# Attention with a threshold and a mixing block on one core: a re-priced plan, joined value products, reciprocals spread through DRAM

## The chip, the cores and the metric

The kernel runs on one core of a Trainium2 chip. The metric is device time in microseconds (us) for the whole program. The core has TensorE (matrix products and transposes, PE in the profile; its weight loads are PEld), VectorE (DVE), ScalarE (ACT), GpSimd (POOL) and SyncE (SP), which here only issues DMAs. Results of TensorE land in PSUM banks; everything else on the chip is in SBUF.

## The reference

Two stages, one behind the other (shapes: 8 batches, 8 heads, 576 positions, 64 per head, so 512 channels):

```python
scores = scale * np.matmul(q, k.transpose(0, 1, 3, 2))
thresh = np.max(scores, axis=-1, keepdims=True) - tau
scores = np.where(scores >= thresh, scores, -1000000000.0)
scores = scores - np.max(scores, axis=-1, keepdims=True)
attn = np.exp(scores)
attn = attn / (np.sum(attn, axis=-1, keepdims=True) + 1e-09)
x = attn @ v                       # heads side by side: 8 x 576 x 512
theta = x @ w_theta
zr = x * np.cos(theta); zi = x * np.sin(theta)
u = x + w_tok_r @ zr + w_tok_i @ zi
out = u + np.maximum(u @ w_ch, 0.0)
```

The weights come in double precision; w_theta and w_tok_i are about five times larger than a usual draw, so the angles need accuracy.

## The kernel before

**Work.** Heads are taken two at a time: 32 pairs, four to a batch. A pair has nine units of 128 rows of scores: four for each head and one that holds the last 64 rows of both (the "tails"). For a unit TensorE makes the scores (s_ps, 128 x 576) from query and key, each split into a high and a low term of a reduced fp32 form (fp32r); VectorE empties them with a minus sign and takes the row minimum (L511), ScalarE takes the exponential (L529), VectorE applies the threshold and sums the rows (L537). TensorE turns the result in blocks of 128 x 128 (t_ps, L572 and L607), ScalarE copies the turned blocks into the tiles a0 (the tails and the first two units of each head, 320 columns) and a1 (256 columns), and TensorE multiplies them with v (o_ps, L650): one run of 20 instructions for a0 in the middle of the pair, one for a1 at its end. ScalarE copies both into x, transposed (xT, channels by positions).

**Normalizing.** The nine columns of row sums of a pair become reciprocals on VectorE (L672, L673). ScalarE spreads eight of them, each over 64 columns (rb, L677); TensorE turns them in four blocks (rb_ps, L685) and the ninth in another (rl_ps, L691), and VectorE multiplies x by what stands in these two banks (L697, and L703 twice).

**Mixing.** For each batch: x is split (xh, xl); the angles are four products of 24 instructions (m_ps, L775); VectorE takes whole turns off; ScalarE makes cosine and sine (L855, L856), for which it loads another table and loads the old one back; GpSimd multiplies by x; TensorE turns z (z_ps, L885), and the token product runs over 4 x 54 instructions (y_ps, L933). Then u is split and multiplied with w_ch (m_ps again).

**Weights.** At the start each block of weights is turned from double precision into a high and a low fp32r term: VectorE works on the bits (L254 to L272), and the low term comes out of TensorE as a sum of three products (w_ps, L301 twice and L302): the bits and a correction w, both as fp32 against an identity (or one divided by a whole turn), minus the high term. There are 8 pieces of 512 columns (w_theta and w_ch) and 18 of 288 (w_tok). The terms of w_theta and w_ch go to DRAM and are read back for each batch (wm).

**Order.** The order on every engine is fixed before the program runs. A planner (class Plan) holds all pieces of work with an engine, a time, what they need, the buffers they take and a rank. It lets time pass: on the engine that can start first it takes, of the works that can start then, the one with the lowest rank. Ranks are counted in steps of 3.2 us a unit, with fixed offsets (a score at h - 3, an exponential at h - 2). Buffers are counted in pots: six PSUM banks, one pair of banks for the scores, three tiles for two units' scores (s2), one each of a0 and a1, three raw tiles. SP issues the DMAs of query, key, their copies (qq, kd, tails), v, weights and outputs in one queue; query and key of a pair are cast on ScalarE after the query was scaled there (L393), the low terms come from GpSimd (for the first pair from VectorE). Each engine runs its list in order, so an instruction that waits holds up all behind it.

## Time and profile before

| | |
|---|---|
| median of 3 runs | 1081.22 us (1077.72 to 1082.82) |
| profiled execution | 1080.86 us, its span 1078.8 us |
| TensorE, VectorE, ScalarE, GpSimd busy | 95%, 74%, 62%, 21% of the span |
| mean granted clock of TensorE | 0.995 |
| DMA engines busy | 49.9% of 16 engines' span |

The span runs from the first to the last instruction of the execution that the profiler recorded; the 2 us beside it lie outside. Matrix products are pipelined: the profile shows the length of one from its own begin to its own end, so what one costs in a row of many is read from the distance between starts.

### The profile page before, as it was taken

How to read it: one execution, taken by the hardware profiler on the slowest of the kernel's cores; microseconds unless marked ns; L12 is line 12 of the kernel's file. 1: busy time of each engine (PE TensorE's matmuls, PEld its weight loads, DVE VectorE, ACT ScalarE, POOL GpSimd, SP SyncE). 2: the span in 40 equal slices, each digit the busy share in tenths (PEclk: the TensorE clock that was granted, in tenths of full speed). 3: DMA queues.
4: the chain of work that ended last, by engine and by line, in shares of the span. 5: the costliest groups of instructions: out<-in, count | busy, mean ns of one | idle time of the engine just before them, and what ended most of it. 6: DMA issues, size and time to landing. Idle time of an engine off the chain costs nothing.

```text
span 1078.8 us, 21076 instructions
## 1 busy us (share of the span) xinstructions
PE 1022.4 (95%) x7650; PEld 905.0 (84%) x7650; DVE 800.1 (74%) x2152; ACT 669.9 (62%) x1269; POOL 231.1 (21%) x162
## 2 busy tenths in 40 slices
PE   4889899998999999999899999999999998999998
PEld 2667688888789988888788987999788888899898
DVE  5998887877777786776777777766877778776572
ACT  5878867645775558655685566754586556854250
POOL 1111232312332014211241123320142212320100
PEclk9999999999999999999999999999999999999999
DMA  8877455556634563346642366444544466421411
GB/s 259 211 211 188 125 135 145 133 161 161 178 89 101 149 168 101 97 101 182 174 117 71 98 187 168 100 101 136 161 118 101 100 180 178 110 59 38 132 54 64
DMA packets 81799, 144.05 MB, mean 134 GB/s; under 512 B 26272, under 2 KB 34464, under 8 KB 81696
## 3 DMA queue, kind: packets, MB, share of 16 engines
q1 hardware_dynamic: 81696, 142.71, 49.9%
q8 instruction: 61, 1.00, 0.4%
q14 instruction: 42, 0.34, 0.1%
HBM read 72.42 MB, written 13.63 MB: 80 GB/s over the span
## 4 chain that ended last, share of the span: by engine, by line
PE 76%; DVE 8%; ACT 7%; DMA 5%; SPq 2%; issue 2%; POOL 0%; ACTq 0%; POOLq 0%; DVEq 0%
PE y_ps L933 22%; PE o_ps L650 13%; PE s_ps L497 12%; PE m_ps L775 12%; PE t_ps L572 9%; PE z_ps L885 3%; DMA qraw<-in_qT_dram 2%; DVE sc L511 2%; PE w_ps L301 2%; DMA kd<-khl 2%; SPq L217 2%; DVE xl L214 1%; PE t_ps L607 1%; DVE s_sb L537 1%; PE rb_ps L685 1%
## 5 line engine op out<-in xcount | busy, mean ns | idle before, releaser
L537 DVE SCALAR_TENSOR_TENSOR s_sb<-sc,nm,s_sb 128x576 f32<-128x576 f32 x288 | 247.1, 863 | 97.8 <-ACT s_sb L529 95.6
L529 ACT ACTIVATE s_sb<-sc,nm 128x576 f32<-128x576 f32 x288 | 223.6, 786 | 85.3 <-DVE sc L511 84.5
L511 DVE TENSOR_SCALAR_CACHE_REDUCE sc<-s_ps 128x576 f32<-128x576 f32 x288 | 216.9, 753 | 57.7 <-PE s_ps L497 56.2
L583 ACT COPY a<-t_ps 128x512 f32<-128x512 f32 x256 | 147.7, 590 | 99.6 <-PE t_ps L572 99.0
L497 PE MATMUL s_ps<-kd,qq 128*128 128x288 f32 x1024 | 186.1, 303 | 22.9 <-DVE sc L511 22.3
L497 PEld LDWEIGHTS s_ps<-kd,qq 128*128 128x128 f32 x1024 | 147.7, 188 | 35.8 <-DVE sc L511 32.1
L572 PE MATMUL t_ps<-ident,s_sb 128*128 128x128 f32 x1152 | 171.9, 274 | 4.5 <-DVE s_sb L537 4.5
L650 PE MATMUL o_ps<-a,v 128*64 128x256 f32 (+1 forms) x1280 | 170.2, 412 | 0.0
L933 PE MATMUL y_ps<-wt_l,zh 128*128 128x288 f32 x576 | 168.0, 308 | 0.0
L933 PE MATMUL y_ps<-wt_h,zh 128*128 128x288 f32 x576 | 163.5, 304 | 0.1
L572 PEld LDWEIGHTS t_ps<-ident,s_sb 128*128 128x128 f32 x1152 | 139.8, 141 | 8.3 <-DVE s_sb L537 6.4
L214 POOL TENSOR_TENSOR qhl<-qraw,qhl 128x576 fp32r<-128x576 f32 x31 | 46.4, 1497 | 460.6 <-ACT qhl L397 380.4
L650 PEld LDWEIGHTS o_ps<-a,v 128*64 128x64 f32 x1280 | 87.8, 137 | 61.2 <-issue 10.6
L933 PE MATMUL y_ps<-wt_h,zl 128*128 128x288 f32 x576 | 114.0, 306 | 0.0
L933 PEld LDWEIGHTS y_ps<-wt_l,zh 128*128 128x128 f32 x576 | 108.1, 189 | 3.7 <-issue 3.7
L933 PEld LDWEIGHTS y_ps<-wt_h,zh 128*128 128x128 f32 x576 | 107.1, 189 | 0.4 <-ACT zh L891 0.4
L775 PE MATMUL m_ps<-xh,wm 128*128 128x288 f32 x512 | 93.1, 307 | 11.3 <-ACT a L583 10.4
L868 POOL TENSOR_TENSOR z<-z,xT 128x576 f32<-128x576 f32 x56 | 78.2, 1432 | 83.4 <-ACT z L855 83.4
L775 PE MATMUL m_ps<-uh,wm 128*128 128x288 f32 x512 | 92.2, 302 | 0.3 <-DVE uh L211 0.3
L933 PEld LDWEIGHTS y_ps<-wt_h,zl 128*128 128x128 f32 x576 | 85.6, 189 | 6.1 <-issue 6.1
L775 PEld LDWEIGHTS m_ps<-xh,wm 128*128 128x128 f32 x512 | 76.0, 193 | 17.1 <-ACT a L583 11.8
L775 PEld LDWEIGHTS m_ps<-uh,wm 128*128 128x128 f32 x512 | 74.6, 188 | 4.3 <-issue 3.8
(88 smaller groups left out, 1440.1 us busy)
## 6 DMA issues: line engine op xcount, KB each, us to landing
wm<-wm_dram SPq DMA_DIRECT2D x64, 512.0 KB, 4.0
kd<-khl SPq DMA_DIRECT2D x64, 288.0 KB, 4.3
qq<-qhl SPq DMA_DIRECT2D x128, 128.0 KB, 2.4
kd<-khl SPq DMA_DIRECT2D x64, 256.0 KB, 4.1
v<-in_vp_dram SPq DMA_DIRECT2D x32, 320.0 KB, 2.9
qraw<-in_qT_dram SPq DMA_DIRECT2D x32, 288.0 KB, 4.4
kraw<-in_kT_dram SPq DMA_DIRECT2D x32, 288.0 KB, 4.7
out_dram<-xT SPq DMA_DIRECT2D x32, 288.0 KB, 4.5
```

The lines of the kernel that those rows point to most:

```text
L214: eng.tensor_tensor(out=out, in0=a, in1=b, op=ALU.subtract)
L497: nc.tensor.matmul(ps.tile[:, half, :HS], st, kk[:, half * HS : (half + 1) * HS], start=(x == 0), stop=(x == len(terms) - 1),)
L511: nc.vector.tensor_scalar(out=sc.tile.rearrange("p (a b) -> p a b", a=2), in0=ps.tile[:, :, :HS], scalar1=-1.0, scalar2=None, op0=ALU.mult ...
L529: nc.scalar.activation(out=u.s.tile[:, j], in_=sc.tile, func=AF.Exp, bias=nm.tile[:, 0:1], scale=-1.0)
L537: nc.vector.scalar_tensor_tensor(out=e, in0=sc.tile, scalar=nm.tile[:, 1:2], in1=e, op0=ALU.is_le, op1=ALU.mult, accum_out=pr.rows.tile[:, ...
L572: nc.tensor.transpose(out=bank.tile[:, c * P : (c + 1) * P], in_=sf[:, k0 + c * P : k0 + (c + 1) * P], identity=ident)
L583: nc.scalar.copy(out=t.a[:, :, j, q0 : q0 + P], in_=bank.tile.rearrange("p (c q) -> p c q", c=4))
L650: nc.tensor.matmul(bank.tile[64 * j : 64 * j + 64, :w], st, mv, start=(c == 0), stop=(c == 4))
L775: nc.tensor.matmul(banks[h].tile[:, :HS], wm.tile[:, a, c, :], x[:, h * HS : (h + 1) * HS], start=(key == 0), stop=(key == 11),)
L868: eng.tensor_tensor(out=zi, in0=zi, in1=xs[m].x.tile, op=ALU.mult)
L885: nc.tensor.transpose(out=bank.tile[:, i * P : (i + 1) * P], in_=z.tile[:, c : c + P], identity=ident)
L933: nc.tensor.matmul(bank.tile[:, :HS], st, (wt_l if wl else wt_h)[:, c, hs], start=(k + q == 0), stop=(k + q == 26),)
```

## The change

- **Planner.** A DMA can start only when at most seven before it are under way (RING), its own time and landing are counted apart; works on VectorE and GpSimd marked "shared" don't run at the same time; each engine may take a work that starts up to SLACK later if its rank is lower; a work may be released before its forerunner's end where only its issue or its first half is needed; times are other numbers throughout. The fixed offsets of ranks are replaced by a table (LEAD). Weights have earlier ranks and closer steps than before.
- **Values.** Both products of a pair are one run of 40 instructions at the pair's end, with two banks. A tile a0 or a1 is taken when the first block is turned for it, not when it is copied.
- **Normalizing.** The nine columns of reciprocals are turned at once (r_ps, 9 x 128), copied to SBUF (rinv), written to DRAM in three DMAs (rows_dram) and read back in two, each over 64 partitions (rb, 128 x 576). One multiplication on VectorE from SBUF takes the place of three.
- **Weights.** The correction w is written as fp32r and multiplied with an fp32r identity. The products of the first batch's token mixing wait for all of w_tok.
- **Start.** The first pair's tails come by two DMAs from ScalarE's queue and are split on ScalarE and VectorE; key is loaded ahead of query; the exponential's table is loaded at once.
- **Scaling.** The factor of the scores sits in VectorE's emptying (scalar1=gate) and no longer in a pass over the query on ScalarE.

```diff
+RING = 8
+SLACK = {"PE": 0.05, "DVE": 0.1, "ACT": 0.1, "POOL": 0.1, "SP": 0.8}
+
+LEAD = dict(
+    score=-4.74, empty=-29.63, offset=-10.18, power=-8.2, mask=12.6, flip=0.34, evict=-7.42, flip5=-4.13,
...
                 first, starts = NEVER, []
+                base = free[e] if e != "SP" else max(free[e], sent[-RING])
                 for w in wait[e]:
-                    at = max(free[e], w.ready)
+                    at = max(base, w.ready)
+                    if w.shared:
+                        at = max(at, port[other[e]])
...
-                    best = (first, min((x for x in starts if x[0] <= first + 1e-6), key=lambda x: x[1].rank)[1])
+                    best = min((x for x in starts if x[0] <= first + SLACK[e]), key=lambda x: x[1].rank)
...
-    PACE, TURN_PACE = 0.131, 0.109
+    PACE, TURN_PACE = 0.1335, 0.109
...
-    nc.vector.tensor_scalar(out=gate, in0=tau_sb, scalar1=0.0, scalar2=1.0 / root, op0=ALU.is_ge, op1=ALU.mult)
+    nc.vector.tensor_scalar(out=gate, in0=tau_sb, scalar1=0.0, scalar2=-1.0 / root, op0=ALU.is_ge, op1=ALU.mult)
...
+    tail_raw = const.tile([P, P], F32, name="tail_raw")
+    nc.gpsimd.memset(tail_raw, 0.0)
+    for j in range(2):
+        r = slice(64 * j, 64 * j + 64)
+        nc.scalar.dma_start(tail_raw[r, r], qT[0, 0, j, :, 512:])
+    nc.scalar.preload_act_table(AF.Exp)
...
+        unit = (turns, turns_r) if turn else (ident, ident_r)
...
-                t.w = get(holds.w, [P, S], F32, "w")[:, :n]
+                t.w = get(holds.w, [P, S], F32R, "w")[:, :n]
...
-            terms = lambda: [t.bits.bitcast(F32), t.w]
+            terms = lambda: [(unit[0], t.bits.bitcast(F32)), (unit[1], t.w)]
...
-        dq = on_sp(load(qr, qT, "qraw"), gate_on, rank, (qr,), 3.0)
-        dk = on_sp(load(kr, kT, "kraw"), gate_on, rank + 0.1, (kr,), 3.0)
-
-        def scale():
-            nc.scalar.activation(out=qr.tile, in_=qr.tile, func=AF.Copy, scale=gate)
+        dk = on_sp(load(kr, kT, "kraw"), gate_on, rank - 0.1, (kr,), 4.2)
+        dq = on_sp(load(qr, qT, "qraw"), gate_on, rank, (qr,), 4.2)
...
-                scalar1=-1.0,
+                scalar1=gate,
...
-        f = on_pe(4, flip, [d3], at(h), (bank,), TURN_PACE)
+        f = on_pe(4, flip, [d3] + t.flips[:1], at(h) + lead("flip"), (bank, t.h) if first else (bank,), TURN_PACE, 0.2)
...
-        if (i, j) in ((1, 1), (3, 1)):
-            values(pr, g, at(h + 1))
+        if k == NU - 1:
+            values(pr, at(h) + lead("values"))
...
+            for g, w in enumerate(widths):
+                t, bank = pr.a[g], banks[g]
+                bank.tile = get(bank, [P, 512], F32, "o_ps")
+                for c in range(5):
+                    for j in range(2):
+                        st = v[:, 4 * j + c, :] if c < 4 else v[:, 8 + j, :]
+                        mv = t.a[:, c, j, :] if c < 4 else t.a5
+                        nc.tensor.matmul(bank.tile[64 * j : 64 * j + 64, :w], st, mv, start=(c == 0), stop=(c == 4))
+
+        need = pr.a[0].evicts + pr.a[1].evicts + [pr.v_in]
...
-            for i in range(4):
-                nc.tensor.transpose(
-                    out=bank.tile[:, i * P : (i + 1) * P], in_=rb.tile[:, i * P : (i + 1) * P], identity=ident
-                )
...
+            bank.tile = get(bank, [P, 512], F32, "r_ps")
+            nc.tensor.transpose(out=bank.tile[:9, :P], in_=pr.rows.tile[:, :9], identity=ident)
+
+        def take():
+            turned.tile = get(turned, [9, P], F32, "rinv")
+            nc.scalar.copy(out=turned.tile, in_=bank.tile[:9, :P])
...
+                if j < 2:
+                    nc.sync.dma_start(
+                        flat.tile[j, 64:].rearrange("(i q) -> i q", q=P), turned.tile[4 * j : 4 * j + 4]
+                    )
+                else:
+                    nc.sync.dma_start(flat.tile[:, :64], turned.tile[8:9].rearrange("o (j q) -> o j q", j=2))
...
+                nc.sync.dma_start(rb.tile[64 * j : 64 * j + 64], flat.tile[j].unsqueeze(0).broadcast_to([64, S]))
...
-            nc.vector.tensor_tensor(out=x[:, 64:], in0=x[:, 64:], in1=bank.tile, op=ALU.mult)
...
+            nc.vector.tensor_tensor(out=x, in0=x, in1=rb.tile, op=ALU.mult)
...
-    rank = 4.0
+    rank = lead("wt")
     for c in range(NM):
         weight_mid(0, w_theta, c, rank)
-        rank += 8.0
+        rank += lead("wt_step")
```

**How the order moves.** First TensorE's list at the program's start (s_ps are scores, khl and tails the terms of key and tails, kd and qq the copies of key and query; w_ps the weights' low terms). Before:

```order
L497 MATMUL s_ps<-khl,tails 128x288 x6
L301 MATMUL w_ps<-bits,turns 128x512
L301 MATMUL w_ps<-w,turns 128x512
L302 MATMUL w_ps<-whi,minus 128x512
L497 MATMUL s_ps<-kd,qq 128x288 x4
```

Now:

```order
L553 MATMUL s_ps<-khl,tails 128x288 x6
L630 MATMUL t_ps<-ident,s_sb 128x128 x4
L666 MATMUL t_ps<-ident,s_sb 128x128
L553 MATMUL s_ps<-kd,qq 128x288 x4
L346 MATMUL w_ps<-bits,turns 128x512
L346 MATMUL w_ps<-w,turns_r 128x512
```

The first unit's turns and the second unit's scores stand ahead of the first weights now, and the correction is multiplied with turns_r.

Second, TensorE's list at the end of the last pair's attention (m_ps from uh and ul is the channel product of the batch before, m_ps from xh and xl the angles of the last batch). Before, where the run of 320 columns ends 17 rows ahead of these:

```order
L691 MATMUL rl_ps<-ident,rows 128x128
L650 MATMUL o_ps<-a_12809,v 64x256 x8
L650 MATMUL o_ps<-a_12810,v 64x256 x2
L775 MATMUL m_ps<-uh,wm_12777 128x288 x4
L685 MATMUL rb_ps<-ident,rb 128x128 x4
L775 MATMUL m_ps<-uh,wm_12777 128x288 x4
L775 MATMUL m_ps<-ul,wm_12777 128x288 x4
L775 MATMUL m_ps<-xh,wm_12924 128x288 x4
```

Now, from the turn of the reciprocals on:

```order
L741 MATMUL r_ps<-ident,rows 9x128
L848 MATMUL m_ps<-ul,wm_11665 128x288 x4
L848 MATMUL m_ps<-ul,wm_11760 128x288 x4
L630 MATMUL t_ps<-ident,s_sb 128x128 x4
L848 MATMUL m_ps<-uh,wm_11760 128x288 x4
L666 MATMUL t_ps<-ident,s_sb 128x128 x2
```

and, behind ten more rows of such products and turns:

```order
L848 MATMUL m_ps<-ul,wm_12739 128x288 x4
L710 MATMUL o_ps<-a_12636,v 64x320 x8
L710 MATMUL o_ps<-a_12637,v 64x320 x2
L710 MATMUL o_ps<-a_12812,v 64x256 x8
L710 MATMUL o_ps<-a_12813,v 64x256 x2
L848 MATMUL m_ps<-xh,wm_12832 128x288 x2
```

The turn of the reciprocals has moved ahead of the pair's last turns of scores, both value products stand together, and between the turn and the first use of x lie 44 products, 18 turns and the value run.

Third, SP's list in the seventh batch (rows_dram is the tile in DRAM, rinv the turned reciprocals, rb what VectorE multiplies by, wm the weights of a mixing product). Before, nothing of the kind stands in it; now:

```order
L405 DMA wm_11562<-wm_dram 128x1024
L432 DMA kraw<-in_kT_dram 128x576
L405 DMA wm_11581<-wm_dram 128x1024
L752 DMA rows_dram_91<-rinv 4x128 x2
L756 DMA rows_dram_91<-rinv 2x1x64
L405 DMA wm_11665<-wm_dram 128x1024
L764 DMA rb<-rows_dram_91 64x576 x2
L405 DMA wm_11760<-wm_dram 128x1024
```

A load of weights, which waits for TensorE to be done with its buffer, stands between the writes and the reads.

## Rows read from the trace of the kernel before

**Rows 1.** The page's head: busy us (share of the span) and number of instructions of each engine, and TensorE's granted clock in 40 slices, in tenths (9 is 90% or more).

```profile
span 1078.8 us, 21076 instructions
PE 1022.4 (95%) x7650; PEld 905.0 (84%) x7650; DVE 800.1 (74%) x2152; ACT 669.9 (62%) x1269; POOL 231.1 (21%) x162
...
PEclk9999999999999999999999999999999999999999
```

**Rows 2.** Busy time of each engine by stretch: the stretch, its length, busy us (x instructions) in the order of the head row, the granted clock, the DMA engines' share and GB/s.

```profile
core 0: us, PE busy (x) PEld busy (x) DVE busy (x) ACT busy (x) POOL busy (x), PEclk, DMA share, GB/s
0.00:16.00 16.00, 2.77 (x8) 2.28 (x9) 6.89 (x19) 6.42 (x9) 0.96 (x7) 1.00 0.79 237
16.00:130.00 114.00, 101.95 (x647) 77.30 (x645) 100.12 (x279) 89.75 (x183) 18.09 (x12) 1.00 0.73 197
...
256.00:382.00 126.00, 121.72 (x944) 109.52 (x946) 94.45 (x259) 80.03 (x151) 30.91 (x21) 1.00 0.50 129
...
760.00:886.00 126.00, 122.17 (x944) 109.94 (x945) 94.68 (x260) 80.69 (x152) 30.77 (x21) 1.00 0.50 130
...
1012.00:1079.00 67.00, 61.47 (x457) 59.61 (x454) 35.88 (x69) 17.44 (x27) 3.04 (x2) 0.99 0.22 71
```

**Rows 3.** The chain that ended last, as shares of the span by engine (PEq, SPq and the like are the engines' queues).

```profile
PE 76%; DVE 8%; ACT 7%; DMA 5%; SPq 2%; issue 2%; POOL 0%; ACTq 0%; POOLq 0%; DVEq 0%
```

**Rows 4.** Who TensorE waited for from 256 to 886 us: total us, times, longest.

```profile
PE s_ps L497 <- DVE sc L511: 10.9, 14, 1.6
PE m_ps L775 <- ACT a L583: 9.0, 5, 1.8
```

**Rows 5.** Timeline of TensorE: start, length of the group, line, operation, out<-in, count; around the two value runs of one pair and its turned reciprocals.

```profile
649.08 0.60 PE L572 MATMUL t_ps<-ident,s_sb 128*128 128x128 f32 x4
649.61 2.91 PE L650 MATMUL o_ps<-a,v 128*64 128x320 f32 x20
652.46 1.32 PE L775 MATMUL m_ps<-xh,wm 128*128 128x288 f32 x8
...
699.34 2.38 PE L650 MATMUL o_ps<-a,v 128*64 128x256 f32 x20
701.65 0.32 PE L691 MATMUL rl_ps<-ident,rows 128*128 128x128 f32 x1
701.81 0.60 PE L685 MATMUL rb_ps<-ident,rb 128*128 128x128 f32 x4
702.17 0.38 PE L933 MATMUL y_ps<-wt_h,zh 128*128 128x288 f32 x1
702.39 0.29 PE L933 MATMUL y_ps<-wt_l,zh 128*128 128x288 f32 x1
```

and from the chain in order of time (start, us, what), a long row of products at the program's end:

```profile
1046.78 13.93 PE y_ps L933 x105
```

**Rows 6.** DMAs: by tile with KB each and median us from issue to landing, and the time of one issue on SP (minimum/median/maximum in ns, first and last start).

```profile
kd<-khl SPq DMA_DIRECT2D x64, 288.0 KB, 4.3
tails<-qhl SPq DMA_DIRECT2D x64, 32.0 KB, 2.2
L217 SPq DMA_DIRECT2D tails<-qhl x64: 597/616/1577, 9.5 to 946.0; - x64
```

**Rows 7.** Timeline of TensorE around a piece of 288 columns and one of 512; a full-precision product shows as two records.

```profile
80.84 0.65 PE L301 MATMUL w_ps<-bits,ident 128*128 128x288 f32 x2
81.33 0.65 PE L301 MATMUL w_ps<-w,ident 128*128 128x288 f32 x2
...
180.08 1.02 PE L301 MATMUL w_ps<-bits,ident 128*128 128x512 f32 x2
180.94 1.02 PE L301 MATMUL w_ps<-w,ident 128*128 128x512 f32 x2
```

**Rows 8.** The start: a row of the chain (start, us, what), then the timeline of all engines (start, us, engine, line, operation; in brackets the idle time before it and what ended it).

```profile
1.18 3.76 DMA qraw<-in_qT_dram
5.02 1.28 ACT L393 ACT_TABLE_LOAD   x1 [5.02 <-DMA qraw<-in_qT_dram]
6.32 0.78 ACT L393 ACTIVATE qraw<-qraw,small 128x576 f32<-128x576 f32 x1
7.00 0.66 ACT L401 CAST khl<-kraw 128x576 fp32r<-128x576 f32 x1
7.68 0.76 DVE L214 TENSOR_TENSOR khl<-kraw,khl 128x576 fp32r<-128x576 f32 x1 [3.55 <-ACT khl L401]
9.53 2.03 SPq L217 DMA_DIRECT2D tails<-qhl  x2
13.23 1.78 PE L497 MATMUL s_ps<-khl,tails 128*128 128x288 f32 x6 [13.23 <-DMA tails<-qhl]
17.71 0.70 PE L497 MATMUL s_ps<-kd,qq 128*128 128x288 f32 x4
```

**Rows 9.** Groups of instructions (busy us, mean ns of one; then the idle time before them), and by source line the minimum/median/maximum in ns: casts and subtractions on VectorE, and GpSimd's multiplication.

```profile
L868 POOL TENSOR_TENSOR z<-z,xT 128x576 f32<-128x576 f32 x56 | 78.2, 1432 | 83.4 <-ACT z L855 83.4
L211 DVE CAST uh<-xT 128x576 fp32r<-128x576 f32 x32 | 15.7, 494 | 0.3
L211 DVE CAST xh<-xT 128x576 fp32r<-128x576 f32 x8 | 9.0, 1131 | 0.0
L214 DVE TENSOR_TENSOR xl<-xT,xh x16: 746/751/1880, 142.2 to 1017.0; 128x576 fp32r<-128x576 f32 x16
L697 DVE TENSOR_TENSOR xT<-xT,rb_ps x32: 675/689/690, 44.4 to 1012.6; 128x512 f32<-128x512 f32 x32
```

336 lines of the change are left out of this document (188 added, 148 removed), and 2 rows, old and new, of the table pots.

## The prediction

> **What bounds the kernel now.** I read the page's busy shares first, then the stretches, the chain, who waits for whom, and last the timeline for prices. TensorE is busy 95% of a span of 1078.8 us, VectorE 74%, ScalarE 62%, at the full granted clock throughout [rows 1]. The stretches show two stages. Up to 130 us only attention and the splitting of the weights run: TensorE starts 13 us late, and from 16 to 130 us it is busy 102.0 of 114 us beside VectorE's 100.1, so there neither has much room. From 256 us a batch takes 126 us, of which TensorE is busy about 122 [rows 2]. The chain that ended last is 76% TensorE, 8% VectorE, 7% ScalarE and 5% DMA [rows 3]. So from 130 us on, each microsecond taken off TensorE's list counts nearly whole; before that only what VectorE lets through. TensorE's own waits in the five batches from 256 to 886 us are few: 10.9 us for a score tile that VectorE has not yet emptied and 9.0 us for a bank still held by a ScalarE copy [rows 4].
>
> **The change part by part,** against the profiled execution's own 1080.9 us (its span and 2 us around it), which lies 0.4 us under the median of 1081.2.
>
> *Reciprocals.* A pair now turns one column (rl) and four blocks (rb): from 701.65 to 701.81 is 0.16 us, to 702.17 another 0.36, and the first product behind them takes 0.22 instead of 0.13, so 0.09 more [rows 5]: 0.61 us. One turn of nine columns stays; I price it as the single rl turn, 0.16. Saved: 0.45 us x 32 pairs = **14.4 us**, all on TensorE, of it 28 pairs behind the first stage. ScalarE's broad copy and two of VectorE's three multiplications go too, on engines with room. What comes instead is five DMAs on SP: three writes and two reads. By the nearest rows: issue 0.62 us each; a write lands like the tails in 2.2 us, a read of 64 partitions like the kd copy in 4.3 [rows 6]. With turn and copy some 0.5 + 3 x 0.62 + 2.2 + 2 x 0.62 + 4.3 = 10 us. What hides them is seen in the new order: the reciprocals depend on the masks alone, so the turn stands ahead of the pair's last transposes. Before the last batch's mixture 44 matrix products of 0.133 us (13.93 us for 105 [rows 5]), 18 transposes of 0.11 and the 5.2 us value run follow it before anything needs the result: 13 us against 10. I take 0 for the latency; if that cover were missing, 7 us a batch.
>
> *Value products.* A run of 256 columns takes 2.31 us, one of 320 takes 2.85 [rows 5]: 0.54 us for 64 columns, so 2.16 for 256 and 0.15 us fixed in each run. Four transposes from 649.08 at 0.11 would end at 649.52, and the run starts at 649.61: 0.09 more on entry, about as much on leaving. Joining two runs saves one such set, at most 0.35 us; at least 0, if the switch of bank inside the run costs the same. I take 0.28, nearer the upper end since the stationary data go on without change of form: x 32 = **9 us**, ends 0 and 11. The price is that both halves of the next pair's turned scores wait for one run at the pair's end.
>
> *Weights' low terms.* The second product of a piece of 288 columns, like the first, is a full-precision one: 0.49 us from its predecessor's start to its own; for 512 columns 0.86 [rows 7]. With operands in the reduced form the kernel's other products use, 288 columns cost 0.133 us, 512 by proportion 0.24. Saved 0.36 x 18 + 0.62 x 8 = 11.5 us. But 22 of the 26 pieces lie before 130 us, where TensorE has 12 us of idle time and VectorE little. The last four count whole (2.5 us), of the others' 9.0 I count a third: **5.5 us**, ends 2.5 and 11.5.
>
> *Start.* TensorE's first product waits at 13.23 us for the tails: query in at 4.94, a table load of 1.28, scaling 0.78, casts, then two DMAs queued behind two others on SP [rows 8]. Now key comes first, tails come over ScalarE's queue, the table loads earlier and the scaling is folded into the emptying. By the same rows: key in at 4.94, cast 0.66, low term 0.76, first product at about 6.5 us, 6.7 earlier; the second score needs kd, 4.3 us after its issue, some 11.5 instead of 17.71. VectorE did weights in the meantime, so not all is won: **4 us**, ends 0 and 6.7.
>
> *The plan.* All order is new: the planner now counts eight DMAs in flight, the lock between VectorE and GpSimd, and longer matrix paces, and its priorities are another table. About 4 us of visible idle time stand in each 126 us stretch [rows 2], 24 us in six. Such a re-ordering can win all of that or double it: ends +24 and -24. I take **8 us**, a third, because what it newly counts is what these rows show: a cast on VectorE that takes 0.49 us elsewhere takes 1.13 at a mixture's start, while GpSimd works [rows 9].
>
> Sum: 14.4 + 9 + 5.5 + 4 + 8 = 40.9 us; 1080.9 - 40.9 = **1040 us**. All good ends give 67.6 us, 1013; all bad ends (12 + 0 + 2.5 + 0 - 24) a loss of 9.5, 1090.
>
> One more thing changes: the multiplication by the reciprocals reads its factor from a tile in SBUF and no longer from a PSUM bank. It took 675 to 690 ns in all 32 cases, while the subtraction xl from two SBUF tiles took 746 to 1880 [rows 9]. The Trainium skill (SBUF — State Buffer, on its shared port pair) says that a VectorE instruction with two SBUF inputs and a GpSimd instruction that reads SBUF exclude each other for the whole instruction, whoever comes second waiting. The spread of xl agrees with that rule, which speaks against this edit; the sum above prices it at nothing, and the fourth rival below has the price if it does count.
>
> **The rivals.**
> 1. *The plan wins much more.* What it newly counts all appears in the trace, and a batch repeats closely: TensorE's busy time in two stretches 504 us apart is 121.7 and 122.2 us [rows 2]. If 20 of the 24 us go and the weights count whole: 14.4 + 9 + 11.5 + 5 + 20 = 60, 1021 us. Against it: in the first stage VectorE stays nearly full.
> 2. *Only the sure part comes.* The gaps only move (single buffers for the turned scores speak for that), the first stage hides weights and start: 14.4 + 9 + 2.5 = 26, 1055 us.
> 3. *The round trip becomes the wait.* SP takes its DMAs in order, and between a pair's three writes and two reads the new order has a load of weights that waits for TensorE. If x arrives late before each mixture, products queued in order behind it stand still. It decides once the stall is over 40.9 / 8 = 5.1 us a batch; with 7 us in eight batches it costs 56, 1096 us, slower than now. Against it: the 13 us of cover.
> 4. *The multiplication waits for GpSimd.* A GpSimd operation takes 1.43 us [rows 9]; for the last pair of each batch, on the path to the mixture, 8 x 1.43 = 11 us: 1051. Against it: GpSimd is busy only 21% of the time [rows 1].
> 5. *The new order wastes what the edits win.* Joined runs make TensorE wait for the pair's last copies; if the idle time in the batches doubles and only the sure part stands against it: 26 - 24 = 2 us, 1079.
>
> **How the numbers follow.** Forecast 50% (its own range 1030 to 1051); rival 1 15%; rival 2 15%; rival 3 7%; rival 4 7%; rival 5 6%. A difference of 0.5%, 5.4 us, is about what a measurement of this kernel can tell from none. Faster: 50 + 15 + 15 + 7 = 87%; same 6% (rival 5); slower 7% (rival 3). The range from 1020 to 1067 takes in the forecast, rivals 2 and 4 and most of rival 1, and leaves rivals 3 and 5 and the best end out.
>
> **What would show it.** Right: TensorE's busy time down by some 30 us with the share still at 94% or more; batches of 120 to 122 us; a value run of about 5.1 us; low-term products of 0.13 and 0.24 us; the first score near 7 us; no wait of VectorE's multiplication on the rb reads beyond a microsecond. Wrong: if TensorE waits for xh or xl at each mixture's start and behind that stands a DMA of rb; if the first mixture starts as late as now although TensorE had less to do; or if the multiplications spread beyond a microsecond. The prediction fails most easily in the term for the plan, which no row prices, only bounds.

## The result and the profile after

The changed kernel takes 1032.21 us (median of 4 runs, 1031.78 to 1035.84) against 1081.9 us before on the same chip: ratio 0.9555, interval 0.9522 to 0.9589, 4.4% faster. The forecast was 1040 us in a range of 1020 to 1067. The profiled execution took 1031.78 us with a span of 1029.7, 49.1 us less than the span of before.

The page's head and its row of the chain, answering to [rows 1, 3]:

```profile
span 1029.7 us, 20745 instructions
...
PE 990.6 (96%) x7496; PEld 885.1 (86%) x7496; DVE 806.0 (78%) x2091; ACT 637.6 (62%) x1238; POOL 243.4 (24%) x162
...
PE 84%; DVE 10%; DMA 2%; issue 2%; ACT 1%; SPq 0%; POOL 0%; ACTq 0%; DVEq 0%; POOLq 0%
```

The stretches, in the columns of [rows 2]:

```profile
core 0: us, PE busy (x) PEld busy (x) DVE busy (x) ACT busy (x) POOL busy (x), PEclk, DMA share, GB/s
0.00:16.00 16.00, 3.48 (x11) 2.44 (x11) 8.17 (x24) 7.06 (x13) 0.85 (x7) 1.00 0.87 232
16.00:130.00 114.00, 93.38 (x549) 68.20 (x551) 100.40 (x261) 80.86 (x165) 16.78 (x10) 0.96 0.75 201
130.00:256.00 126.00, 124.31 (x944) 110.54 (x942) 103.52 (x273) 83.11 (x162) 33.66 (x22) 1.00 0.59 162
256.00:382.00 126.00, 125.77 (x987) 113.43 (x984) 101.49 (x260) 79.91 (x158) 35.36 (x23) 1.00 0.55 154
...
760.00:886.00 126.00, 126.00 (x986) 113.14 (x985) 99.53 (x259) 78.85 (x153) 33.07 (x22) 1.00 0.51 141
```

TensorE is now busy for the whole of a stretch in the batches: 125.77 and 126.00 of 126 us, where 121.72 and 122.17 stood before, and it issues 987 and 986 products in that time instead of 944. In the first stage it is the other way round: from 16 to 130 us it does less work than before (93.38 instead of 101.95 us) in the same time, at a granted clock of 0.96 instead of 1.00, beside a VectorE that is as full as it was (100.40 against 100.12). Behind its first product and up to 130 us it waits mostly for VectorE and for the copies of q (total us, times, longest):

```profile
PE s_ps L553 <- DVE sc L567: 9.9, 14, 1.3
PE s_ps L553 <- DMA qq<-qhl: 6.4, 2, 3.9
PE t_ps L630 <- DVE s_sb L593: 5.3, 5, 2.8
```

From 256 to 886 us, against the 19.9 us of [rows 4], only one row of TensorE's waits is left:

```profile
PE m_ps L848 <- DMA wm<-wm_dram: 0.2, 1, 0.2
```

To see where 49.1 us come from, I cut both timelines of TensorE at the first product of a mixture (m_ps<-xh), once a batch. Up to the second mixture the kernel before takes 261.89 us, the changed one 260.80: 1.1 us won. The five batches from there to the seventh mixture take 126.15 us each before (to 892.66) and 118.33 after (to 852.47): 7.82 us won in each, 39.1 in all. The rest, with one more batch and the tail, takes 186.1 and 177.2: 8.9 us. So nearly all of the gain is made in the batches, at an even rate, and almost none in the first stage. (The first mixture starts later than before, at 128.7 us instead of 118.5; its place in TensorE's list moves with the order.) For one batch, each group counted from its start to the next group's start, with the idle time set apart (us, mean of the five batches):

| TensorE, us a batch | before | after | two value runs again | four turns more |
|---|---|---|---|---|
| idle before a group | 3.98 | 0.05 | 0.73 | 0.17 |
| reciprocals' turns (rl, rb; after: r) | 2.15 | 0.11 | 0.19 | 1.86 |
| value products o_ps | 20.65 | 20.01 | 20.61 | 20.01 |
| scores s_ps | 21.09 | 20.91 | 20.97 | 20.76 |
| turned scores t_ps | 15.00 | 14.50 | 14.71 | 14.28 |
| m_ps, y_ps, z_ps together | 63.29 | 62.76 | 62.97 | 63.12 |
| batch | 126.15 | 118.33 | 120.18 | 120.20 |

Of the 7.82 us, 3.93 are idle time, 2.04 the reciprocals, 0.64 the value products, and 1.2 small shifts between the other groups. (The last two columns belong to experiments below.) Some of those shifts are the clock: before, the granted clock fell twice in these five batches, and once behind them, to 0.72 in the 6 us from 412, 665 and 917 us, each time behind a pause of TensorE of 1.4 to 1.8 us (nine other pauses of 1.6 to 1.8 us were followed by no fall); in the changed kernel it is 1.00 all through the batches. Each fall is (1 - 0.72) x 6 = 1.7 us, by estimate, so two of them make 0.7 us a batch. The first of the three, by stretch:

```profile
412.00:418.00 6.00, 5.25 (x32) 4.55 (x34) 3.77 (x11) 4.91 (x11) 2.59 (x2) 0.72 0.19 73
```

Two edits can be read directly. First TensorE's timeline in the columns of [rows 5], at a value run and at the turn of the nine columns:

```profile
312.24 0.69 PE L553 MATMUL s_ps<-kd,qq 128*128 128x288 f32 x4
312.77 0.27 PE L741 MATMUL r_ps<-ident,rows 128*9 128x128 f32 x1
312.80 0.38 PE L1012 MATMUL y_ps<-wt_l,zh 128*128 128x288 f32 x1
313.01 0.30 PE L1012 MATMUL y_ps<-wt_h,zh 128*128 128x288 f32 x1
...
318.20 5.07 PE L710 MATMUL o_ps<-a,v 128*64 128x320 f32 x40
323.20 0.66 PE L630 MATMUL t_ps<-ident,s_sb 128*128 128x128 f32 x4
```

The joined run takes 5.00 us from its start to the next group; the two of before took 2.85 and 2.31 [rows 5], so 0.16 us go for a pair. The turn takes 0.03 us from its start to the next product's, but that product then takes 0.21 instead of 0.13 us. Over the 24 pairs behind the second mixture the means are 0.027 us and 0.084 more for the next product, so a turn costs 0.11 us in all, and 0.34 us a batch of the 2.04 in the table comes back in the groups behind the turns. Then the issue of the DMAs that bring the reciprocals and the multiplication by them, by source line (minimum/median/maximum in ns), and what VectorE waited for ahead of the multiplication:

```profile
L764 SPq DMA_DIRECT2D rb<-rows_dram x64: 468/526/2218, 56.4 to 959.6; - x64
...
L770 DVE TENSOR_TENSOR xT<-xT,rb x32: 746/758/762, 61.2 to 967.2; 128x576 f32<-128x576 f32 x32
...
  ACT xT L721: 56.9, 27
```

The last row gives ScalarE's copy of the values, not the DMA: the round trip through DRAM is never what VectorE waits for here. And all 32 multiplications lie between 746 and 762 ns.

The start, in the columns of [rows 8]:

```profile
2.71 1.28 ACT L249 ACT_TABLE_LOAD   x1 [2.71 <-issue]
...
6.28 0.67 ACT L445 CAST khl<-kraw 128x576 fp32r<-128x576 f32 x1
...
6.99 0.61 PE L553 MATMUL s_ps<-khl,tails 128*128 128x288 f32 x1 [6.99 <-ACT khl L445]
...
17.29 1.06 PE L553 MATMUL s_ps<-kd,qq 128*128 128x288 f32 x3 [3.85 <-DMA qq<-qhl]
```

The first product starts 6.2 us earlier (6.99 instead of 13.23), the second score tile only 0.4 us (17.29 instead of 17.71): it waits for the copies of q, as a row of the chain in order of time (start, us, what) shows:

```profile
10.14 7.02 DMA qq<-qhl
```

That copy takes 7 us from its issue until TensorE is released, at a DMA share of 0.87 in the first 16 us. The same row has 4.70 to 6.38 us in the traces of experiments 1, 2, 3 and 5.

### The profile page after: what moved, and what is told of

It is laid out like the page before. It is cut to its first block, busy times and chain, and to the rows that moved or that the text cites. A ratio compares the mean times of both kernels' runs of the same rounds, so it can differ in the third digit from the quotient of the medians.

```text
span 1029.7 us, 20745 instructions
## 1 busy us (share of the span) xinstructions
PE 990.6 (96%) x7496; PEld 885.1 (86%) x7496; DVE 806.0 (78%) x2091; ACT 637.6 (62%) x1238; POOL 243.4 (24%) x162
## 4 chain that ended last, share of the span: by engine, by line
PE 84%; DVE 10%; DMA 2%; issue 2%; ACT 1%; SPq 0%; POOL 0%; ACTq 0%; DVEq 0%; POOLq 0%
PE y_ps L1012 21%; PE m_ps L848 19%; PE s_ps L553 15%; PE o_ps L710 14%; PE t_ps L630 10%; DVE s_sb L593 3%; PE z_ps L962 3%; DVE sc L567 3%; PE t_ps L666 2%; DMA qq<-qhl 1%; PE w_ps L346 1%; DVE bits L308 1%; DMA wm<-wm_dram 1%; DVE w L317 0%; DVE mag L313 0%
## 5 line engine op out<-in xcount | busy, mean ns | idle before, releaser
L567 DVE TENSOR_SCALAR_CACHE_REDUCE sc<-s_ps,small 128x576 f32<-128x576 f32 x288 | 234.6, 815 | 61.2 <-PE s_ps L553 57.6
L593 DVE SCALAR_TENSOR_TENSOR s_sb<-sc,nm,s_sb 128x576 f32<-128x576 f32 x288 | 255.8, 897 | 21.0 <-ACT s_sb L585 18.7
L641 ACT COPY a<-t_ps 128x512 f32<-128x512 f32 x256 | 150.4, 589 | 115.8 <-PE t_ps L630 114.7
L553 PEld LDWEIGHTS s_ps<-kd,qq 128*128 128x128 f32 x1024 | 149.9, 190 | 24.6 <-DVE sc L567 13.0
L1012 PE MATMUL y_ps<-wt_h,zh 128*128 128x288 f32 x576 | 167.5, 308 | 0.0
L710 PE MATMUL o_ps<-a,v 128*64 128x256 f32 (+1 forms) x1280 | 164.7, 413 | 0.0
L943 POOL TENSOR_TENSOR z<-z,xT 128x576 f32<-128x576 f32 x56 | 80.8, 1470 | 182.0 <-ACT z L928 182.0
L1012 PE MATMUL y_ps<-wt_h,zl 128*128 128x288 f32 x576 | 110.7, 304 | 0.0
L258 POOL TENSOR_TENSOR khl<-kraw,khl 128x576 fp32r<-128x576 f32 x31 | 51.5, 1661 | 244.3 <-DMA out_dram<-xT 102.3
L721 ACT COPY xT<-o_ps 128x320 f32<-128x320 f32 x64 | 25.6, 399 | 120.3 <-PE o_ps L710 120.3
```

What stands on the lines that cost most here:

```text
L258: eng.tensor_tensor(out=out, in0=a, in1=b, op=ALU.subtract)
L553: nc.tensor.matmul(ps.tile[:, half, :HS], st, kk[:, half * HS : (half + 1) * HS], start=(x == 0), stop=(x == len(terms) - 1),)
L567: nc.vector.tensor_scalar(out=sc.tile.rearrange("p (a b) -> p a b", a=2), in0=ps.tile[:, :, :HS], scalar1=gate, scalar2=None, op0=ALU.mult ...
L593: nc.vector.scalar_tensor_tensor(out=e, in0=sc.tile, scalar=nm.tile[:, 1:2], in1=e, op0=ALU.is_le, op1=ALU.mult, accum_out=pr.rows.tile[:, ...
L641: nc.scalar.copy(out=t.a[:, :, j, q0 : q0 + P], in_=bank.tile.rearrange("p (c q) -> p c q", c=4))
L710: nc.tensor.matmul(bank.tile[64 * j : 64 * j + 64, :w], st, mv, start=(c == 0), stop=(c == 4))
```

## The experiments

Each kernel was timed in three rounds beside the kernel before on the same chip, and it is the ratio to before that is compared. For each, the table has the cuts from the trace as above: the start of the second mixture, the mean of the five batches from there, and what follows.

| kernel | ratio to before, interval | second mixture, us | a batch, us | rest, us |
|---|---|---|---|---|
| before | 1 | 261.9 | 126.15 | 186.1 |
| changed | 0.9555 [0.9522, 0.9589] | 260.8 | 118.33 | 177.2 |
| 1 full low terms | 0.9552 [0.9536, 0.9567] | 264.0 | 118.28 | 177.1 |
| 2 fixed factor | 0.9480 [0.9456, 0.9504] | 258.4 | 118.12 | 177.0 |
| 3 four turns more | 0.9640 [0.9624, 0.9657] | 265.6 | 120.20 | 179.0 |
| 4 first loads fewer | 0.9546 [0.9514, 0.9578] | 263.1 | 118.44 | 177.3 |
| 5 a hair (control) | 0.9517 [0.9490, 0.9544] | 258.1 | 118.23 | 177.0 |
| 6 old offsets | 0.9816 [0.9790, 0.9842] | 268.1 | 124.50 | 180.8 |
| 7 old model | 0.9839 [0.9813, 0.9865] | 266.9 | 122.48 | 183.1 |
| 8 scaling on ScalarE | 0.9509 [0.9487, 0.9530] | 257.0 | 118.38 | 178.2 |
| 9 no shared port | 0.9702 [0.9666, 0.9738] | 270.6 | 120.25 | 179.3 |
| 10 no queue of eight | 0.9511 [0.9465, 0.9557] | 257.8 | 118.38 | 177.4 |
| 11 no slack | 0.9652 [0.9618, 0.9686] | 265.5 | 120.21 | 179.2 |
| 12 two value runs | 0.9743 [0.9707, 0.9779] | 275.1 | 120.18 | 180.3 |

**1. The weights' low terms in full precision again**, in the same order of instructions.

```diff
-                t.w = get(holds.w, [P, S], F32R, "w")[:, :n]
+                t.w = get(holds.w, [P, S], F32, "w")[:, :n]
-        unit = (turns, turns_r) if turn else (ident, ident_r)
+        unit = (turns, turns) if turn else (ident, ident)
```

> The changed kernel in its own order, with the weights' correction w and its identity in fp32 again, so that 26 products take 0.49 or 0.86 us in place of 0.13 or 0.24 (11.5 us of TensorE in all, 2.5 us of it behind the first stage). Theory: up to the first mixture VectorE and the first loads set the pace and TensorE has room, so the saving was hidden: 1032 to 1037 us. Rival: the low terms lie on the path: 1042 to 1045 us.

Measured: 0.9552, the changed kernel's own ratio to 0.0003. TensorE's timeline has the work back: a piece of 288 columns takes 1.10 us here (55.43 to 56.53) and 0.75 in the changed kernel (55.20 to 55.95):

```profile
55.43 0.65 PE L346 MATMUL w_ps<-bits,ident 128*128 128x288 f32 x2
55.91 0.65 PE L346 MATMUL w_ps<-w,ident 128*128 128x288 f32 x2
56.18 0.51 PE L347 MATMUL w_ps<-wt_h,minus 128*128 128x288 f32 x1
56.53 0.65 PE L346 MATMUL w_ps<-bits,ident 128*128 128x288 f32 x2
```

and in the changed kernel:

```profile
55.20 0.65 PE L346 MATMUL w_ps<-bits,ident 128*128 128x288 f32 x2
55.47 0.51 PE L346 MATMUL w_ps<-w,ident_r 128*128 128x288 f32 x1
55.82 0.29 PE L347 MATMUL w_ps<-wt_h,minus 128*128 128x288 f32 x1
55.95 0.65 PE L346 MATMUL w_ps<-bits,ident 128*128 128x288 f32 x2
```

So the single price was right (0.35 us a piece; 0.36 was forecast), but the times show nothing of it and the trace 3.2 us, by which the second mixture starts later. Up to the second mixture the products w_ps take 28.4 us of TensorE's timeline in the changed kernel, 38.5 here and 37.3 before, and its idle time is 27.8, 25.5 and 14.6: most of what the products saved turned into waiting. One thing blurs this: here the granted clock is 1.00 from 16 to 130 us, and in the changed kernel it is 0.96 (see the last section), so the two first stages differ by more than the edit.

**2. The emptying of the scores with a constant** instead of the factor read from SBUF, same order.

```diff
-                scalar1=gate,
+                scalar1=-0.125,
```

> The changed kernel in its own order; the emptying of a score tile multiplies by the number -0.125 in the instruction and no longer by a factor read from SBUF (so the case of a negative tau is left out). In the changed kernel's trace that instruction takes 815 ns on average, before it took 753. Theory: reading the factor costs these 60 ns, and only the first stage, which VectorE fills, feels it: the mean falls back to about 753 ns, some 40 units there give 2 to 3 us: 1029 to 1031 us. Rival A: the 60 ns come from the new order (VectorE held up by GpSimd): the mean stays near 815 and the time at 1032. Rival B: VectorE bounds the batches too: 288 x 0.06 = 17 us, 1015 us.

Measured: 0.9480, 8 us below the changed kernel by the ratios, 3.7 by the spans of the profiled executions (1026.0 and 1029.7). The group's mean falls from 815 to 755 ns, so 60 ns x 288 = 17 us of VectorE go; here and in the changed kernel:

```profile
L567 DVE TENSOR_SCALAR_CACHE_REDUCE sc<-s_ps 128x576 f32<-128x576 f32 x288 | 217.3, 755 | 65.8 <-PE s_ps L553 61.5
```

```profile
L567 DVE TENSOR_SCALAR_CACHE_REDUCE sc<-s_ps,small 128x576 f32<-128x576 f32 x288 | 234.6, 815 | 61.2 <-PE s_ps L553 57.6
```

In the batches almost nothing comes of it (118.12 against 118.33): there VectorE has room. What is won, 2.4 us, is won before the second mixture. The theory's 2 to 3 us agree with the trace, and the 8 us of the ratio lie above them.

**3. Four turns more for each pair**, behind the turn of the reciprocals.

```diff
             nc.tensor.transpose(out=bank.tile[:9, :P], in_=pr.rows.tile[:, :9], identity=ident)
+            for i in (1, 2, 3, 1):
+                nc.tensor.transpose(out=bank.tile[:, i * P : (i + 1) * P], in_=ident, identity=ident)
```

> The changed kernel with four more turns of 128 columns in front of every pair's next work on TensorE, right behind the turn of the reciprocals (nobody reads them); all else in the same order. It puts back the TensorE time that spreading the reciprocals through DRAM took away (0.44 us a pair), without the rest. Theory: behind the first stage TensorE is full, so 28 pairs pay whole and four are hidden: 12 us more, 1044 us (1042 to 1047). Rival: TensorE has slack between its works and the turns vanish in it: 1032 to 1036 us.

Measured: 0.9640, 9 us over the changed kernel by the ratios, 15.9 by the spans of the profiled executions (1045.6 and 1029.7; the first is of the slowest of four, the second of the fastest). In the batches 16 turns more cost 1.86 - 0.11 = 1.75 us in the ledger above, 0.109 us a turn, and the batch grows by 1.87. So in the batches TensorE's work counts in full, microsecond for microsecond, which is what the whole forecast was built on. 0.44 us a pair is what was taken away, and 0.43 is what the ledger shows as saved, (2.04 - 0.34) / 4. The second mixture starts 4.8 us later, though the turns up to it add only 3.7 us. So the early turns were not hidden, as the theory had four pairs of them; part of the 4.8 us may be the clock, at 0.94 from 16 to 130 us.

**4. Fewer loads ahead of the first copies of q**: v of the first pair and q and k of the second are loaded only after the first pair's q copies have been issued (planned anew).

```diff
+        if n == 1:
+            gate_on = [pairs[0].q_in[0][1]]
         dk = on_sp(load(kr, kT, "kraw"), gate_on, rank - 0.1, (kr,), 4.2)
...
+        if n == 0:
+            gate_on = [pr.q_in[0][1]]
         pr.v_in = on_sp(load_v, gate_on, at(NU * n) + lead("prep") + 6, (pr.v,), 3.0)
```

> The changed kernel, but v of the first pair and query and key of the second are loaded only when the first pair's copies of query and key have been issued, so 0.9 MB less stand ahead of these; the plan is made anew. In the changed kernel the first product starts at 7.0 us, the second unit's scores only at 17.3 us, when a copy of the query that was issued at about 10 us has landed. Theory: full DMA queues at the start are what ate the gain of the early first product: the second unit's scores start 3 to 5 us earlier and the time falls by 2 to 4 us, to 1028 to 1030 us. Rival: VectorE's work for the weights fills that time anyway: scores earlier, time at 1031 to 1034 us.

Measured: 0.9546, no gain, and the second mixture at 263.1 us. The second unit's scores do start earlier, at 14.96 us instead of 17.29, with a DMA share of 0.75 instead of 0.87 up to 16 us; that is the rival of the expectation. The loads at the start are not what holds up the first stage; with experiment 1 that points at VectorE, 100 of 114 us busy. This is inferred. Experiment 2 takes VectorE's work away, and its second mixture comes 2.4 us earlier, but the next control moves it as far.

**5. A control**: one number of the planner moved by a hair, so that works whose times almost tie change places.

```diff
-    PACE, TURN_PACE = 0.1335, 0.109
+    PACE, TURN_PACE = 0.1336, 0.109
```

> The changed kernel with one number of the planner moved by a hair (a product's step on TensorE 0.1336 instead of 0.1335 us), which reorders works whose times almost tie. It is the control for all runs that are planned anew: a difference to the changed kernel below the one seen here says nothing. If the order is robust: ratio 0.952 to 0.960 (within 5 us of 1032). If the offsets were fitted so tightly that any new tie spoils them: 5 to 20 us slower, ratio 0.960 to 0.974. The batches of 117.6 us stay within 0.5 us in the first case.

Measured: 0.9517, batches of 118.23. The order is robust in the batches (0.1 us), while the second mixture moves by 2.7 us and the ratio by 0.0038, 4 us. Below that the ratios of the other runs say nothing on their own, and I read them by the cuts of the trace. The 117.6 us a batch of the expectations is not what these cuts give for the changed kernel, 118.33. Experiment 2 kept the order, so this is not its control; but of its 8 us only 3.7 stand in the trace, and the rest is of the size that moves here.

**6. The old due times** in the planner, with the corrected model.

```diff
-    score=-4.74, empty=-29.63, offset=-10.18, power=-8.2, mask=12.6, flip=0.34, evict=-7.42, flip5=-4.13,
+    score=-3, empty=-5, offset=-4, power=-2, mask=-1.5, flip=0.0, evict=-2, flip5=0.03,
...
```

> The changed kernel, planned with the due times of before in place of the 35 new offsets; the corrected model stays (queue of eight, shared port, slack, new durations). Theory 1 (the offsets won back the 4 us of TensorE's idle in each batch): six steady batches of 120.5 to 122 us instead of 117.6, 1050 to 1062 us, ratio 0.970 to 0.982. Rival (the corrected model won it, and the offsets only fine-tune): within 6 us of the changed kernel, ratio below 0.962. Second rival (with the new durations the old due times fit worse than before): over 1065, ratio above 0.985.

Measured: 0.9816, 28 us over the changed kernel, as theory 1 had it; batches of 124.50, above its 120.5 to 122, and the second mixture at 268.1. The profiled execution is the slowest of five (1073.2 us, median 1064.9) and the one with the lowest mean clock (0.977 against 0.980 to 0.989), so the times taken from it are too long, by 8 us in all; a batch of the median execution is nearer to 123.5, by estimate. The trace shows one event in every batch. All engines around the mixture at 268 us (start, us, engine, line, operation):

```profile
264.37 3.58 POOL L258 TENSOR_TENSOR xl<-xT,xh 128x576 fp32r<-128x576 f32 x2 [4.51 <-ACT xh L253]
...
264.70 1.95 DVE L770 TENSOR_TENSOR xT<-xT,rb 128x576 f32<-128x576 f32 x1
...
266.58 0.80 DVE L567 TENSOR_SCALAR_CACHE_REDUCE sc<-s_ps,small 128x576 f32<-128x576 f32 x1
...
267.44 0.80 PE L553 MATMUL s_ps<-kd,qq 128*128 128x288 f32 x4 [1.83 <-DVE sc L567]
```

and TensorE's clock there (stretches, columns as above):

```profile
262.00:268.00 6.00, 4.17 (x35) 3.92 (x34) 5.41 (x11) 5.03 (x11) 3.58 (x2) 1.00 0.77 226
268.00:274.00 6.00, 5.50 (x26) 5.18 (x26) 5.53 (x14) 2.53 (x4) 0.00 (x0) 0.55 0.42 99
274.00:280.00 6.00, 6.00 (x43) 6.00 (x43) 3.42 (x11) 0.13 (x1) 0.00 (x0) 0.88 0.43 114
```

The multiplication by the reciprocals falls beside GpSimd's subtraction and takes 1.95 us instead of 0.75; the emptying behind it is late, TensorE stands still for 1.83 us, and the granted clock then falls to 0.55, so that in the 6 us from 268 on 26 products run where about 47 do otherwise (987 in 126 us). So the pauses here, 1.83 and 0.51 us, cost some three more in the clock: (1 - 0.55) x 6 + (1 - 0.88) x 6 = 3.4 us. The same stands at 390.85 us with 1.96 us and a clock of 0.57 from 394 on; of the 32 multiplications 7 fall beside GpSimd, one for each mixture from the second on. The clock doesn't fall every time: the pause of 1.85 us at 889.9 is followed by none. This is the mechanism of the prediction's fourth rival, not in the changed kernel but in one with the same instructions and other due times.

**7. The three new rules of the planner off**, with the new due times.

```diff
-RING = 8
-SLACK = {"PE": 0.05, "DVE": 0.1, "ACT": 0.1, "POOL": 0.1, "SP": 0.8}
+RING = 800
+SLACK = {"PE": 1e-6, "DVE": 1e-6, "ACT": 1e-6, "POOL": 1e-6, "SP": 1e-6}
...
+        shared = False
```

> The changed kernel with the three new rules of the planner off (no queue of eight for DMAs, no exclusion of VectorE and GpSimd, no slack in the choice), and with the new offsets, durations and instructions. Theory 1 (offsets): within 8 us of the changed kernel, ratio 0.954 to 0.963, the batches at 118 to 119 us; the xh cast on VectorE is again stretched beside GpSimd's subtractions (mean over 700 ns instead of 456) but VectorE is not the bound, so that costs little. Rival (model): 15 to 30 us slower, ratio 0.969 to 0.983, with idle of TensorE of 3 us or more per batch and waits on VectorE behind it.

Measured: 0.9839, 31 us over the changed kernel, so the rival of that expectation held, at the upper end of its range, and theory 1 fell. A batch has 2.99 us of idle time on TensorE again. Its waits of TensorE from 256 to 886 us:

```profile
PE t_ps L667 <- DVE s_sb L594: 5.6, 5, 1.4
PE s_ps L554 <- DVE sc L568: 4.8, 9, 1.2
PE r_ps L742 <- DVE rows L738: 4.3, 5, 0.9
```

All three are waits on VectorE. The granted clock is 1.00 from 256 to 886 us all the same, so these shorter pauses cost no more than their length. What I had expected to see beside them, a cast stretched beside GpSimd, is not there: the xh cast takes 455 ns.

**9, 10 and 11. One rule off at a time.** Each is one line of experiment 7's edit: the shared port, the queue, the slack.

> The changed kernel, planned without the one rule that VectorE and GpSimd exclude each other (the queue of eight and the slack stay). Theory 1 (the rule keeps VectorE's operations of two SBUF operands from being stretched just where TensorE waits for them): half or more of the 33 us that the old model cost, ratio 0.967 to 0.984, the xh cast on VectorE over 700 ns instead of 456. Rival (the offsets fit only the choice made with the slack): within 8 us of the changed kernel, ratio 0.952 to 0.961, even if single casts are stretched.

> The changed kernel, planned without the queue of eight outstanding DMAs. The order on TensorE is nearly that of the changed kernel except ahead of the first mixture. Theory 1 (a small part): ratio 0.951 to 0.960, the batches within 0.5 us of 117.6, a difference only up to the second mixture (258 to 268 us). Rival (the queue is what the planner had to know): 10 us or more slower, ratio over 0.962, with TensorE waiting for DMAs in the batches.

> The changed kernel, planned without the slack (an engine takes the earliest work even where one with an earlier due time could start 0.05 to 0.1 us later; SyncE 0.8). Theory 2 (due times only count where several works are ready together, so without slack the offsets lose their hold): half or more of the 33 us of the old model, ratio 0.967 to 0.984, batches of 119.5 to 122. Rival (slack decides little, the shared port was the cost): within 8 us of the changed kernel, ratio 0.952 to 0.961.

Measured: without the shared port 0.9702 (16 us over the changed kernel), without the slack 0.9652 (10 us), without the queue 0.9511 (no difference to the control). The two that count add up to 26 of the 31 us. The slack's ratio lies between the ranges of its theory and its rival, so it decides neither. For the shared port theory 1 had the right number. But the mechanism that I gave for the first isn't what happens: in that run the multiplications all take 757 ns and the xh cast 456, as in the changed kernel, and the masks that have GpSimd at work for over 0.3 us of their time are 52 of 288 there and 57 in the changed kernel. Only the uh casts differ: six fall beside GpSimd in either kernel, and take 1.28 to 1.32 us without the rule and 0.87 to 0.90 with it, 2.5 us of VectorE in all. So most of the 16 us does not come from operations that the rule keeps from being stretched. What is left is that it gives another order, and the offsets were fitted for the order with it; the same may be said of the slack. That the fit is the cause is argued, not shown. Whether the rules have a worth of their own, with due times fitted without them, was not tried.

**8. The scaling on ScalarE again**, and the emptying with -1.0: a kernel that does all the work and would be the better one if experiment 2's gain were real.

```diff
-                scalar1=gate,
+                scalar1=-1.0,
...
+        def scale():
+            nc.scalar.activation(out=qr.tile, in_=qr.tile, func=AF.Copy, scale=gate)
...
-        a2 = on_act(0.58, q_high, [dq], rank, (ql,))
+        a1 = on_act(0.68, scale, [dq], rank)
+        a2 = on_act(0.58, q_high, [a1], rank, (ql,))
```

> The changed kernel, with q scaled on ScalarE again before the split (32 instructions of about 0.68 us, and one of the tails), and the emptying of the scores with the constant -1.0 again, planned anew. Computes all that the reference does. Theory (the factor read from SBUF costs VectorE 62 ns in each of 288 emptyings, of which the run with a fixed factor gave back 8 us; ScalarE at 62% takes the 22 us of scaling without loss): 4 to 9 us faster than the changed kernel, ratio 0.947 to 0.952; the mean of the emptying is back to 755 ns. Rival (the 8 us came from the start of the kernel, where the scaling again stands in the chain to the first scores): within 3 us of the changed kernel, ratio 0.953 to 0.958, with the second mixture not before 260 us.

Measured: 0.9509, 5 us below the changed kernel but level with the control; the emptying is at 755 ns again, the batches at 118.38, the second mixture at 257.0. So it is not shown to be better: the numbers lie within what a new order of ties does.

**12. The value products as two runs again**, at their old places, planned anew.

```diff
-        if k == NU - 1:
-            values(pr, at(h) + lead("values"))
+        if (i, j) in ((1, 1), (3, 1)):
+            values(pr, g, at(h) + lead("values"))
```

> The changed kernel with the value products of a pair as two runs again, at the places where they stood before (one behind the score tiles of the first two row blocks, one at the pair's end), planned anew with the new offsets. By the trace of the changed kernel the joined run takes 5.0 us against 2.84 and 2.31 with their entries: 0.32 us for each of 32 pairs, 10 us in all, so ratio 0.960 to 0.966 (theory: the joining is worth its measured time, the TensorE being the bound), batches of 119 us (4 pairs of 0.32 more than 117.6). Rival 1 (the early run filled pauses that the joined one leaves): 0.950 to 0.957, no slower. Rival 2 (the offsets were fitted to the joined run): over 0.970, with new idle in the batches.

Measured: 0.9743, 20 us over the changed kernel: above the theory's range, and where the second rival has it (over 0.970, with new idle time in the batches). The ledger parts it. The runs themselves are as before, from the timeline:

```profile
305.95 2.38 PE L709 MATMUL o_ps<-a,v 128*64 128x256 f32 x20
308.26 0.33 PE L666 MATMUL t_ps<-ident,s_sb 128*128 128x128 f32 x1
...
320.82 2.91 PE L709 MATMUL o_ps<-a,v 128*64 128x320 f32 x20
323.66 0.28 PE L737 MATMUL r_ps<-ident,rows 128*9 128x128 f32 x1
```

2.31 and 2.84 us, together 0.15 more than the joined run: 0.60 us a batch. The batch grows by 1.85, the other 1.25 being idle time (0.68) and shifts; and the second mixture comes 14 us later. So the joining by itself is worth 0.15 us x 32 = 5 us. The remaining 15 are idle time, shifts and a lower clock in the first stage (0.96 up to the second mixture, where the changed kernel has 0.98); that an order whose due times were fitted to the joined run is the reason is the likely reading, not shown.

## Why the prediction was right, and where its terms were not

The time lies 8 us under the forecast and inside its own narrower range (1030 to 1051). That it lies so near is in part luck: values, weights and start were too high by some 11 to 14 us together, the plan too low by 20 or more, and the two errors went against each other. Carried to the end, the same ledger gives 48.0 us from the second mixture on: 24.3 of 24.8 us of idle time, 10.1 for the reciprocals (with what comes back in the products behind the turns), 4.1 for the value products, and 9.5 for everything else, of which some 5 are the three falls of the clock. By its steps:

- **What bounds the kernel.** Right, and shown by experiment 3: from the second mixture on TensorE's work counts whole. Right also that ahead of it work saved counts little: TensorE was busy 8.6 us less from 16 to 130 us, and the second mixture starts 1.1 us earlier. But it read the clock as full throughout from slices of 27 us that show 9 for 90% or more; behind the first stage of the kernel before it fell three times, and these 5 us are in no term.
- **Reciprocals, 14.4 us.** Right: 1.7 us a batch, 0.43 a pair against 0.45 forecast; the 24 pairs behind the second mixture give 10.1 us, all 32 would give 13.7. The turn that stays costs 0.11 us with what it adds to the next product, not 0.16. The latency, taken as 0, is 0: no row of VectorE's waits names the DMA, so the third rival, 1096 us, falls.
- **Value products, 9 us.** The mechanism is right and the size was off: 0.15 to 0.16 us a pair, not 0.28, 5 us. Only the fixed part of a run (0.15 by the working) was saved; the entry and the exit that were added to it did not show up as savings of the runs.
- **Weights' low terms, 5.5 us.** The price of a piece was right to 0.01 us; the share of it that counts was not: a third of the early pieces was taken and nothing can be seen in the times, 3 us in the trace (experiment 1, whose first stage ran at a higher clock). The four late pieces, counted whole, are within that.
- **Start, 4 us.** The working of the first product holds (6.99 us, 6.5 forecast), that of the second tile doesn't: 17.29, not 11.5. The step that failed is that it needs only kd; it waits for the copies of q too, which are issued behind those of key and took 7.0 us instead of the 4.3 of [rows 6], at a DMA share of 0.87; that was not in the sum. Nor would the rest have counted: experiment 4 has this tile 2.3 us earlier and no gain. The term is 0, as far as the traces show.
- **Plan, 8 us.** The term that was mis-sized. All of the idle time in the batches went, not a third: 3.93 us a batch of 3.98, 24.3 us to the end, just the bound of 24. On top of it come the 9.5 us in the other groups, some 5 of them the falls of the clock, which the bound left out; how much of these 9.5 is the plan's is open. Taking the plan back costs 28 us (old due times) and 31 us (old rules), but either is charged with the loss of the fit as well. Neither the due times nor the rules win it alone: each without the other gives 1062 to 1065 us, 7 to 10 us above what the second rival had for the sure part (1055). The reason given for the term doesn't explain it: the xh cast beside GpSimd [rows 9] is gone (all eight take 452 to 460 ns), but it is gone in experiments 7 and 9 too (455 and 456), which are 31 and 16 us slower. And the first stage gave some back: it lost 5.1 us of clock that the kernel before did not lose there.
- **The rivals.** The first (the plan wins 20 us) is the nearest in mechanism: it had the plan right and the weights and the start too high, so that its 1021 lies 11 us under the result as the forecast lies 8 above. The fourth (the multiplication waits for GpSimd) does not happen in this order, all 32 taking 746 to 762 ns, but experiment 6 shows that it is a matter of order alone. The second (the gaps only move) falls, as 0.05 us of idle time a batch are left. The fifth (the order wastes the gains) was 47 us off. Of the third's 7 us a batch the prediction shows no working.
- **Its signs.** TensorE's busy time fell by 31.8 us (30 were named), the first score came at 6.99 us and a value run took 5.00; a batch fell to 118.3, below the 120 to 122. One sign of being wrong did appear: the first mixture starts 10.2 us later, though TensorE had less to do. It tells little, since in experiment 4 it starts at 156.3 us and the time is the same.

One cost was not in the prediction at all: folding the scaling into the emptying makes that instruction read its factor from SBUF and take 815 ns instead of 753 in the mean, 62 ns x 288 = 17.9 us more on VectorE. It was hidden, as VectorE is busy 100 of 126 us in the batches. With TensorE at 126 of 126 us now, the next gain in the batches has to come from TensorE's own work; ahead of them TensorE waits for VectorE, for the copies of q and loses some of its clock, and which of these would pay was not tried beyond the 2.4 us of experiment 2.

## What to carry to other kernels

Where one engine is near full, price its work by the start of one group to the start of the next and count it whole, but only in the stretches where nothing else is as full: work saved where the engine then waits for another is worth little until that other is relieved too. The idle time of the bound engine is worth more than its length where its clock falls behind the pauses, as in experiment 6; in experiment 7 it did not. A table of due times is fitted to one set of instructions and planner's rules; an edit or a rule that is judged by taking it out of a fitted order is charged with the loss of the fit, so part the ledger (its own groups, idle time, other stages) before putting a price on it.
